# Gated MLP on groups of four token tiles: gate and up matmuls of 512 columns, with tanh and key masks in place

## Chip, cores, metric

One core of a Trainium2 chip (trn2). The metric is device time of one execution in microseconds, the median over runs; lower is better.

## The reference, cut to what matters

Two layers, each of sliding-window attention (32 heads of 16, window 256) and a gated MLP, on 2048 tokens of width 512, in bf16:

```python
def _B_ref(x, w_gate, w_up, w_down):          # F = 1792
    g = x @ w_gate
    u = x @ w_up
    return (sigmoid(g) * u) @ w_down

x = x + A(layernorm(x)); x = x + B(layernorm(x))   # twice, with the same weights
```

The kernel computes sigmoid(g)·u as 0.5·(tanh(g/2) + 1)·u, the 0.5 being applied after the down projection.

## The kernel before

The kernel does not write its instructions in a loop nest. A list scheduler in Python, run once when the kernel is built, plays the engines through with estimated durations and emits each instruction when its turn comes. What remains on the chip is one fixed order for each engine, with semaphores between them. Numbers for tuning (priorities, paces, ranks, slacks) steer that scheduler. TensorE's work comes as "units" that each own one of four PSUM banks until they are evacuated; between them go the "visits" of the attention (scores into a separate buffer, one exponential of 128x2048 each) and the values. The rest, all projections and the gated MLP, is called dense below. xnT is the normalized input and OnT the attention output, both transposed, mostly by DMA, for the matmuls that read them.

The gate and up unit took one or two token tiles of 128. Gate and up shared a bank, 256 columns each:

```python
def gate_up_unit(self, L, t0, n, fcs, chunk):            # n = 1 or 2 tiles
    def steps(bank):
        pt = self.banks[bank][:].rearrange("p (i f w) -> p i f w", i=2, w=w)      # w = n * 128
        return [... nc.tensor.matmul(pt[:, i, j, :], lhsT=wt[:, kt, fc * P:(fc + 1) * P],
                    rhs=self.xnT[key][0][:, c0 // P:(c0 + w) // P, kt, :], start=kt == 0, stop=kt == KT - 1)
                for i, wt in enumerate((self.wg, self.wu)) for j, fc in enumerate(fcs) for kt in range(KT)]
    def evac(u):
        def tanh(e):
            box["th"] = self.take("th")                                           # ring of 3
            nc.scalar.activation(out=box["th"][0][:], in_=pt[:, 0, :], func=AF.Tanh, scale=0.5)
        def mult(e):
            nc.vector.scalar_tensor_tensor(out=self.hT[:, chunk, :], in0=box["th"][0][:], scalar=1.0,
                                           in1=pt[:, 1, :], op0=ALU.add, op1=ALU.mult)
# ... cut
```

Keys were copied from PSUM into one of two `kt` buffers and from there masked into a padded key buffer, once for the even and once for the odd heads:

```python
def cp(e):
    box["kt"] = self.take("kt")
    self.copy(e, box["kt"][0][:], self.banks[u.bank][:])
def split(e):
    for i in range(2):
        nc.vector.tensor_scalar(out=self.kTp[gi % 2][:, cq, :, i, :], in0=box["kt"][0][:]..., scalar1=self.rms[i][:, 0:1], ...)
```

The softmax here doesn't subtract the row's maximum and nothing guards it: scores larger than these inputs give would overflow.

## Time and profile before

| | kernel before |
|---|---|
| time, median of 3 (first measurement) | 545.37 us (545.32 to 545.83) |
| span of the profiled execution | 544.5 us |
| TensorE matmul / weight load / VectorE / ScalarE busy | 98 / 65 / 77 / 72 % |
| granted TensorE clock | full |
| TensorE instructions: matmuls, weight loads | 11,068 of each |

Two groups of the page matter besides (line, engine, operation, output<-input, shapes, count | busy us, mean ns of one | idle time before, and what ended it); they are the evacuation of the gate and up banks in the kernel before:

```profile
L817 ACT ACTIVATE th<-bank 128x256 bf16<-128x256 f32 x224 | 80.6, 386 | 61.6 <-PE bank L805 58.0
L820 DVE SCALAR_TENSOR_TENSOR hT<-th,bank 128x256 bf16<-128x256 bf16 x224 | 87.7, 415 | 36.8 <-ACT th L817 36.0
```

ScalarE stands idle for 58.0 us in total until TensorE has a gate bank ready, and VectorE for 36.0 us until the tanh is there. Neither engine is what TensorE works towards; they follow it.

### The profile page before, as it was taken

How to read it: one execution, taken by the hardware profiler on the slowest of the kernel's cores; microseconds unless marked ns; L12 is line 12 of the kernel's file. 1: busy time of each engine (PE TensorE's matmuls, PEld its weight loads, DVE VectorE, ACT ScalarE, POOL GpSimd, SP SyncE). 2: the span in 40 equal slices, each digit the busy share in tenths (PEclk: the TensorE clock that was granted, in tenths of full speed). 3: DMA queues.
4: the chain of work that ended last, by engine and by line, in shares of the span. 5: the costliest groups of instructions: out<-in, count | busy, mean ns of one | idle time of the engine just before them, and what ended most of it. 6: DMA issues, size and time to landing. Idle time of an engine off the chain costs nothing.

```text
span 544.5 us, 24319 instructions
## 1 busy us (share of the span) xinstructions
PE 534.5 (98%) x11068; PEld 354.8 (65%) x11068; DVE 420.6 (77%) x902; ACT 394.5 (72%) x455; POOL 45.3 (8%) x105
## 2 busy tenths in 40 slices
PE   8999999999999999999999999999999999999997
PEld 7446754866667565665667656766667576777874
DVE  6998989787989889899878877886666867554432
ACT  3999879878889787788878877786878875422321
POOL 6301100010101010001100001010000000000000
PEclk9999999999999999999999999999999999999999
DMA  8852233232313271345111621136111422310000
GB/s 272 312 137 91 42 72 52 63 42 53 61 43 42 52 109 26 60 88 73 37 37 42 109 43 35 35 54 104 42 42 38 85 60 49 63 40 10 12 22 29
DMA packets 94903, 36.41 MB, mean 67 GB/s; under 512 B 78160, under 2 KB 93776, under 8 KB 94800
## 3 DMA queue, kind: packets, MB, share of 16 engines
q1 hardware_dynamic: 93440, 33.56, 29.2%
q8 instruction: 86, 1.41, 1.0%
q10 hardware_dynamic: 1360, 1.31, 0.8%
q14 instruction: 17, 0.14, 0.1%
HBM read 9.70 MB, written 2.10 MB: 22 GB/s over the span
## 4 chain that ended last, share of the span: by engine, by line
PE 91%; DVE 3%; DMA 3%; ACT 2%; issue 1%; POOL 0%; ACTq 0%; POOLq 0%
PE bank L805 35%; PE bank L838 17%; PE bank L1082 9%; PE Sps L1002 7%; PE bank L865 5%; PE bank L713 5%; PE bank L742 5%; PE bank L778 4%; DMA xnT<-xn 2%; PE Sps L1013 2%; PE bank L1265 1%; ACT PTring L1055 1%; ACT edge L1055 1%; DVE edge L933 1%; DMA OnT<-On 1%
## 5 line engine op out<-in xcount | busy, mean ns | idle before, releaser
L1055 ACT ACTIVATE PTring<-Sps 128x2048 bf16<-128x2048 f32 (+1 forms) x122 | 225.9, 1852 | 45.0 <-PE Sps L1002 41.8
L805 PE MATMUL bank<-xnT,wg 128*128 128x256 bf16 (+1 forms) x1064 | 138.1, 256 | 1.4 <-DMA xnT<-xn 0.8
L805 PE MATMUL bank<-xnT,wu 128*128 128x256 bf16 (+1 forms) x1064 | 139.1, 256 | 0.0
L817 ACT ACTIVATE th<-bank 128x256 bf16<-128x256 f32 x224 | 80.6, 386 | 61.6 <-PE bank L805 58.0
L820 DVE SCALAR_TENSOR_TENSOR hT<-th,bank 128x256 bf16<-128x256 bf16 x224 | 87.7, 415 | 36.8 <-ACT th L817 36.0
L838 PE MATMUL bank<-wd,hT 128*128 128x512 bf16 x448 | 115.3, 380 | 0.0
L805 PEld LDWEIGHTS <-wg 128*128 128x128 bf16 x1064 | 89.3, 98 | 28.0 <-issue 2.7
L805 PEld LDWEIGHTS <-wu 128*128 128x128 bf16 x1064 | 90.6, 98 | 11.4 <-issue 0.6
L1055 ACT ACTIVATE edge<-Sps 128x2048 bf16<-128x2048 f32 (+1 forms) x32 | 56.7, 1772 | 12.9 <-PE Sps L1013 12.9
L838 PEld LDWEIGHTS <-hT 128*128 128x128 bf16 x448 | 41.5, 98 | 34.0 <-issue 0.8
L933 DVE TENSOR_TENSOR PTring<-PTring,mask 128x1024 bf16<-128x1024 bf16 x64 | 43.9, 687 | 22.5 <-ACT PTring L1055 22.3
L1082 PE MATMUL bank<-PTring,Vaug 128*32 128x64 bf16 (+1 forms) x2880 | 52.2, 203 | 0.5 <-issue 0.5
L1002 PEld LDWEIGHTS <-kTp 32*128 32x128 bf16 x1984 | 25.6, 93 | 41.0 <-issue 39.2
L1082 PEld LDWEIGHTS <-Vaug 128*32 128x32 bf16 x2880 | 44.1, 97 | 9.7 <-issue 6.4
L1002 PE MATMUL Sps<-qT,kTp 32*128 32x64 bf16 (+3 forms) x1984 | 47.9, 214 | 2.1 <-ACT PTring L1055 2.0
L621 POOL TENSOR_SCALAR st<-st 128x2 f32<-128x2 f32 (+1 forms) x37 | 11.2, 303 | 431.6 <-DVE st L616 431.6
L615 DVE BATCH_NORM_STATS2 st<-xsb 128x6 f32<-128x512 bf16 x64 | 43.9, 686 | 2.1 <-DMA xsb<-in_A_x_dram 1.7
L1082 PE MATMUL bank<-edge,Vl 128*32 128x64 bf16 x1024 | 44.5, 193 | 0.0
L681 DVE CAST OTs<-bank 128x512 bf16<-128x512 f32 x51 | 37.1, 729 | 9.0 <-PE bank L1082 8.8
L933 DVE TENSOR_TENSOR edge<-edge,maske 128x1024 bf16<-128x1024 bf16 x60 | 40.6, 682 | 4.1 <-ACT edge L1055 3.9
L1082 PE MATMUL bank<-edge,Vh 128*32 128x64 bf16 x896 | 40.8, 193 | 0.0
L933 DVE TENSOR_TENSOR PTring<-PTring,maskn 128x1024 bf16<-128x1024 bf16 x56 | 38.1, 682 | 0.7 <-ACT PTring L1055 0.7
(71 smaller groups left out, 527.5 us busy)
## 6 DMA issues: line engine op xcount, KB each, us to landing
Vl<-Vaug SPq DMA_DIRECT2D x32, 68.0 KB, 2.8
out_dram<-xsb SPq DMA_DIRECT2D x16, 128.0 KB, 2.1
Vh<-Vaug SPq DMA_DIRECT2D x28, 68.0 KB, 2.8
wg<-in_B_w_gate_dram SPq DMA_DIRECT2D x2, 896.0 KB, 10.1
wu<-in_B_w_up_dram SPq DMA_DIRECT2D x2, 896.0 KB, 12.8
wd<-in_B_w_down_dram SPq DMA_DIRECT2D x7, 256.0 KB, 4.7
xsb<-in_A_x_dram SPq DMA_DIRECT2D x6, 256.0 KB, 7.0
wq<-in_A_wqkv_dram ACTq DMA_DIRECT2D x2, 256.0 KB, 4.7
```

The source lines that it names most:

```text
L615: nc.vector.bn_stats(out=st[:, 0:6], in_=self.xsb[:, t, :])
L681: self.nc.vector.tensor_copy(out=out, in_=in_)
L713: return [(mm_ns(w), lambda kt=kt, o=o: nc.tensor.matmul(self.banks[bank][:, o:o + w], lhsT=self.wq[:, kt, cq * P:cq * P + P], rhs=self.xn ...
L742: return [(mm_ns(w), lambda kt=kt, o=o: nc.tensor.matmul(self.banks[bank][:, o:o + w], lhsT=self.wq[:, kt, D + cq * P:D + cq * P + P], rhs ...
L805: return [(mm_ns(w), lambda i=i, j=j, fc=fc, wt=wt, kt=kt: nc.tensor.matmul(pt[:, i, j, :], lhsT=wt[:, kt, fc * P:(fc + 1) * P], rhs=self. ...
L817: nc.scalar.activation(out=box["th"][0][:], in_=pt[:, 0, :], func=AF.Tanh, scale=0.5)
L820: nc.vector.scalar_tensor_tensor(out=self.hT[:, chunk, :], in0=box["th"][0][:], scalar=1.0, in1=pt[:, 1, :], op0=ALU.add, op1=ALU.mult)
L838: nc.tensor.matmul(self.banks[bank][:], lhsT=self.hT[:, c, o:o + P], rhs=self.wd[:, fc, :], start=fc == 0, stop=fc == FC - 1)
L933: done = pl.task({"DVE": dve_bf_ns(1024)}, lambda e: nc.vector.tensor_tensor(out=r, in0=r, in1=m.to_broadcast([P, 16, HP]), op=ALU.mult), ...
L1002: nc.tensor.matmul(self.sps[:, m, o:o + n * HP], lhsT=kTp[32 * m:32 * m + 32, i, tt, e, :], rhs=self.qT[32 * m:32 * m + 32, i, q0:q0 + n * ...
L1055: nc.scalar.activation(out=out, in_=src, func=AF.Exp, scale=scale)
L1082: nc.tensor.matmul(o, lhsT=Va[:, c0:c0 + 32], rhs=p(h), start=k == 0 or t == 0, stop=k == len(parts) - 1 or t == 0, tile_position=(0, 32 * g))
```

## The change

The intent: matmuls of 512 columns for gate and up, so that each weight load serves four token tiles. Gate and up then fill a bank each. The tanh is written straight into hT and multiplied there; the key copy goes straight into the padded key buffer and is masked there. Both free buffers, and hT grows from 16 to 28 chunks of 256. The tuning numbers were set anew. Cut to its core:

```diff
-GT = 2
-GW = GT * P
-HCH = 16
+GW = 2 * P
+HCH = 28
+KS = 8
+GLU = [[[1] * 4 + [4], [1] * 4 + [2] * 2, ...], [..., [4] * 4]]     # tiles per group; g0=1, g2=2 choose
-PACE = [2621, 3006, 2091, 2676, 22]
+PACE = [2621, 3006, 2055, 2786, 22]
 ... PRIO, SLACK, RANK, LATE_PRIO, LATE_SLACK, LATE_RANK: new numbers (cut)
-        self.kTp = [big.tile([P, NCQ, NBG, 2, P], BF16, name=f"kTp{i}") for i in range(2)]
+        self.kTp = big.tile([P, NCQ, KS, 2, P], BF16, name="kTp")
-        self.hT = big.tile([P, HCH, GW], BF16, name="hT")
+        self.hT = big.tile([P, HCH * GW], BF16, name="hT")
-        ring("kt", 2, [P, TGW])
-        ring("th", 3, [P, GW])
@@ keys
-                self.copy(e, box["kt"][0][:], self.banks[u.bank][:])
+                    self.copy(e, self.kTp[:, cq, at:at + n, 0, :], self.banks[u.bank][:]...)
-                for i in range(2):
-                    nc.vector.tensor_scalar(out=self.kTp[gi % 2][:, cq, :, i, :], in0=box["kt"][0][:]..., ...)
+                    for i in (1, 0):
+                        nc.vector.tensor_scalar(out=kt[:, :, i, :], in0=kt[:, :, 0, :], ...)
@@ gate and up
+            def tanh(...): nc.scalar.activation(out=self.hT[:, ch[0] * GW:ch[0] * GW + size], in_=pt, func=AF.Tanh, scale=0.5)
+            def mult(...): h = self.hT[:, ...]; nc.vector.scalar_tensor_tensor(out=h, in0=h, scalar=1.0, in1=pt, ...)
+            # four tiles: two units, one bank each
+            units.append(Unit(kind, lambda bank, fcs=fcs: mms(bank, (self.wg,), fcs), needs, True, gate))
+            units.append(Unit(kind, lambda bank, fcs=fcs: mms(bank, (self.wu,), fcs), [], False, up))
```

More of the change, by code (lines that the diff above doesn't have):

```diff
@@ L98 @@
 EXP_NS = 1880
-PACE = [2621, 3006, 2091, 2676, 22]
+GLU = [[[1] * 4 + [4], [1] * 4 + [2] * 2, [1] * 6 + [2], [1] * 8], [[4] * 3 + [2, 1, 1], [4] * 3 + [2, 2], [4] * 4]]
+PACE = [2621, 3006, 2055, 2786, 22]
 EARLY = 12
@@ L113 @@
 FETCH = (1200, 2300)
-PRIO = dict(st_x0=8.84, ap_x0=5.2, xt_x0=4.11, st_x1=6.83, ap_x1=4.97, xt_x1=-3.99, st_x=7.22, ap_x=1.33,
-    xt_x=-1.25, st_p=4.93, ap_p=3.21, xt_p=4.95, st_g=6.44, ap_g=2.28, xt_g=4.79, st_g0=1.93, ap_g0=1.06,
-    xt_g0=2.83, tp=5.29, tp_g=-1.09, q=6.35, q0=3.12, q1=2.88, k=3.53, k0=2.42, k1=4.8, s=-1.61, s0=0.46,
-    s1=0.69, v=-0.71, v0=3.45, v1=8.0, vv=2.2, exp=4.44, exp0=4.73, m0=4.61, m00=-2.03, e0=2.88, e00=6.59,
-    e1=-0.82, e10=4.98, m2=0.81, m20=21.82, th=1.67, mu=-0.98, dn=0.66, add=6.3, add0=5.49, out=5.31, mv=6.94,
-    mv0=3.86, oq=4.47, oq0=3.3, no=1.9, no0=2.41, on=-0.26, on0=4.14, vc=2.28, vc0=5.62)
@@ L122 @@
-OPT = dict(gu='SP', g1=1, bk=1, bq=1, wide=0, r0=2)
-SLACK = dict(xt=1080, oq=1057, on=696, vc=1992)
-RANK = dict(tp=-0.355, o=1.872, lead=10.494, far=6.876, v=1.959, g=2.363, d=3.317, feed=15.682, x3=44361,
-    wd=380, go=211)
-LATE_PRIO = dict(st_p=4.07, ap_p=5, xt_p=3.41, st_x=1.67, ap_x=2, xt_x=-0.8, st_g=2.98, ap_g=0.63, xt_g=2,
-    q=3.84, k=3, s=3, v=3, exp=3, m0=4.57, e0=1.63, e1=6, m2=6.84, th=0.66, mu=1, dn=1.45, add=0.69, out=5.87,
-    mv=5.22, oq=0.1, no=4, on=2, vc=3.04)
-LATE_SLACK = dict(xt=0, oq=0, on=345, vc=0)
@@ L130 @@
-LATE_RANK = dict(tp=-2, o=-1, lead=10, far=5.293, v=4, g=1.974, d=2.5, feed=12, go=300)
+PRIO = dict(st_x0=9.66, ap_x0=5.2, xt_x0=4.11, st_x1=6.83, ap_x1=4.97, xt_x1=-3.99, st_x=7.22, ap_x=1.33,
+    xt_x=-1.25, st_p=4.93, ap_p=3.21, xt_p=5.11, st_g=6.44, ap_g=2.28, xt_g=4.67, st_g0=1.93, ap_g0=2.34,
+    xt_g0=2.83, tp=5.29, tp_g=-2.14, q=6.35, q0=1.85, q1=2.88, k=3.53, k0=0.63, k1=0.73, s=-1.61, s0=0.46,
+    s1=5.56, v=-1.31, v0=3.84, v1=8.0, vv=4.71, exp=4.44, exp0=6.15, m0=4.27, m00=-2.03, e0=3.94, e00=6.05,
+    e1=4.23, e10=4.3, m2=0.81, m20=21.82, th=2.08, mu=-0.98, dn=2.02, add=5.32, add0=5.49, out=5.31, mv=6.36,
+    mv0=3.86, oq=6.63, oq0=3.3, no=0.56, no0=0.37, on=-0.26, on0=4.14, vc=4.31, vc0=-2.12)
@@ new lines @@
+OPT = dict(gu='SP', g1=1, bk=1, bq=1, wide=0, r0=2, g0=1, g2=2)
+SLACK = dict(xt=1080, oq=240, on=28, vc=2480)
+RANK = dict(tp=-2.963, o=1.872, lead=10.494, far=6.876, v=1.959, g=2.363, d=3.317, feed=14.564, x3=44361,
+    wd=12, go=211)
+LATE_PRIO = dict(st_p=4.07, ap_p=2.35, xt_p=6.18, st_x=1.67, ap_x=5.19, xt_x=-0.8, st_g=2.98, ap_g=1.19,
+    xt_g=5.62, q=3.84, k=3, s=3, v=0.28, exp=3, m0=4.62, e0=1.63, e1=6, m2=6.84, th=3.38, mu=3.54, dn=2.85,
+    add=0.69, out=5.87, mv=5.22, oq=0.1, no=4, on=1.28, vc=3.04)
@@ L134 @@
+LATE_SLACK = dict(xt=0, oq=1051, on=203, vc=0)
+LATE_RANK = dict(tp=-2, o=1.5, lead=10, far=5.293, v=1.796, g=1.974, d=2.466, feed=22.042, go=1418)
 class Late(dict):
@@ L732, in q_unit, with k_slots @@
         return u
+    def k_slots(self, j, n):
+        a = min(n, KS - j % KS)
+        return [(0, a, j % KS)] + ([(a, n - a, 0)] if n > a else [])
     def k_unit(self, L, g, cq):
@@ L746, in evac @@
         def evac(u):
-            box = {}
             u.done.then(lambda: self.used(key, 1))
+            slots = self.k_slots(gi * NBG, NBG)
             def cp(e):
-                box["kt"] = self.take("kt")
-                self.copy(e, box["kt"][0][:], self.banks[u.bank][:])
+                for a, n, at in slots:
+                    self.copy(e, self.kTp[:, cq, at:at + n, 0, :], self.banks[u.bank][:].rearrange("p (t k) -> p t k", k=P)[:, a:a + n, :])
             def split(e):
-                for i in range(2):
-                    nc.vector.tensor_scalar(out=self.kTp[gi % 2][:, cq, :, i, :], in0=box["kt"][0][:].rearrange("p (t k) -> p t k", k=P),
-                                            scalar1=self.rms[i][:, 0:1], scalar2=None, op0=ALU.mult)
-            a = pl.task({"ACT": act_ns(TGW), "DVE": dve_ns(TGW)}, cp, [u.done], self.prio["k" + self.phase(L, g)], lambda: self.has("kt"))
-            b = pl.task({"DVE": 620}, split, [a.done], self.prio["s" + self.phase(L, g)], port=True)
-            b.done.then(lambda: (self.give(box["kt"]), self.k_ready[L, g, cq].fire()))
+                for a, n, at in slots:
+                    kt = self.kTp[:, cq, at:at + n]
+                    for i in (1, 0):
+                        nc.vector.tensor_scalar(out=kt[:, :, i, :], in0=kt[:, :, 0, :], scalar1=self.rms[i][:, 0:1], scalar2=None, op0=ALU.mult)
+            a = pl.task({"ACT": act_ns(TGW), "DVE": dve_ns(TGW)}, cp, [u.done], self.prio["k" + self.phase(L, g)])
+            b = pl.task({"DVE": 300 + 320 * len(slots)}, split, [a.done], self.prio["s" + self.phase(L, g)], port=True)
+            b.done.then(self.k_ready[L, g, cq].fire)
             return a.done
@@ L765, in k_unit @@
         needs = [self.has_wq["k"]] + ([] if by_tile else tiles)
-        if gi >= 2:
-            needs.append(self.seen[divmod(4 * (gi - 2) + 3, NT)])
+        if gi * NBG + NBG > KS:
+            needs.append(self.seen[divmod(gi * NBG + NBG - 1 - KS, NT)])
         u = Unit(("k", L, g, cq), steps, needs, False, evac)
@@ L796, in v_unit @@
         return Unit(("v", L, t), steps, needs, False, evac)
-    def gate_up_unit(self, L, t0, n, fcs, chunk):
-        nc, pl, key = self.nc, self.pl, ("g", L, t0 // NBG)
-        c0, w = (t0 % NBG) * P, n * P
-        def steps(bank):
-            pt = self.banks[bank][:].rearrange("p (i f w) -> p i f w", i=2, w=w)
-            return [(mm_ns(w), lambda i=i, j=j, fc=fc, wt=wt, kt=kt: nc.tensor.matmul(
-                pt[:, i, j, :], lhsT=wt[:, kt, fc * P:(fc + 1) * P], rhs=self.xnT[key][0][:, c0 // P:(c0 + w) // P, kt, :],
-                start=kt == 0, stop=kt == KT - 1))
-                for i, wt in enumerate((self.wg, self.wu)) for j, fc in enumerate(fcs) for kt in range(KT)]
-        def evac(u):
-            box = {}
-            u.done.then(lambda: self.used(key, 1))
-            pt = self.banks[u.bank][:].rearrange("p (i w) -> p i w", i=2)
-            def tanh(e):
-                box["th"] = self.take("th")
-                nc.scalar.activation(out=box["th"][0][:], in_=pt[:, 0, :], func=AF.Tanh, scale=0.5)
-            def mult(e):
-                nc.vector.scalar_tensor_tensor(out=self.hT[:, chunk, :], in0=box["th"][0][:], scalar=1.0, in1=pt[:, 1, :],
-                                               op0=ALU.add, op1=ALU.mult)
-            a = pl.task({"ACT": act_ns(GW)}, tanh, [u.done], self.prio["th"], lambda: self.has("th"))
-            b = pl.task({"DVE": dve_ns(GW)}, mult, [a.done], self.prio["mu"])
-            b.done.then(lambda: (self.give(box["th"]), [self.h_ready[L, t0, fc].fire() for fc in fcs]))
-            return b.done
-        needs = [self.xn_ready[key, t] for t in range(t0, t0 + n)] + [self.has_gu]
-        needs.append(self.h_free[chunk])
-        self.h_free[chunk] = self.h_used[L, t0, fcs[-1]]
-        return Unit(("g", L, t0, fcs[0]), steps, needs, True, evac)
@@ L833, in down_unit, with glu_units, mms, tanh @@
-    def down_unit(self, L, t, t0, n, chunks):
+    def glu_units(self, L, t0, n, c0):
+        key, kind = ("g", L, t0 // NBG), ("g", L, t0)
+        q0, w = t0 % NBG, n * P
+        per = GW // w if n < NBG else 1
+        def mms(bank, wts, fcs):
+            pt = self.banks[bank][:, 0:len(wts) * len(fcs) * w].rearrange("p (i f w) -> p i f w", i=len(wts), w=w)
+            return [(mm_ns(w), lambda i=i, j=j, fc=fc, wt=wt, kt=kt: self.nc.tensor.matmul(
+                pt[:, i, j, :], lhsT=wt[:, kt, fc * P:(fc + 1) * P], rhs=self.xnT[key][0][:, q0:q0 + n, kt, :],
+                start=kt == 0, stop=kt == KT - 1))
+                for i, wt in enumerate(wts) for j, fc in enumerate(fcs) for kt in range(KT)]
+        units = []
+        for at, f in enumerate(range(0, FC, per)):
+            fcs = list(range(f, f + per))
+            ch = [(c0 + at * (w * per // GW) + i) % HCH for i in range(w * per // GW)]
+            box = {"got": Event()}
+            needs = [self.xn_ready[key, t] for t in range(t0, t0 + n)] + [self.has_gu]
+            for c in ch:
+                needs.append(self.h_free[c])
+                self.h_free[c] = self.h_used[L, t0, fcs[-1]]
+            size = w * per
+            def tanh(pt, box, done, ch=ch, size=size):
+                def fn(e):
+                    self.nc.scalar.activation(out=self.hT[:, ch[0] * GW:ch[0] * GW + size], in_=pt, func=AF.Tanh, scale=0.5)
+                a = self.pl.task({"ACT": act_ns(size)}, fn, [done], self.prio["th"])
+                a.done.then(box["got"].fire)
+                return a.done
+            def mult(pt, box, done, fcs=fcs, ch=ch, size=size):
+                def fn(e):
+                    h = self.hT[:, ch[0] * GW:ch[0] * GW + size]
+                    self.nc.vector.scalar_tensor_tensor(out=h, in0=h, scalar=1.0, in1=pt, op0=ALU.add, op1=ALU.mult)
+                b = self.pl.task({"DVE": dve_ns(size)}, fn, [done, box["got"]], self.prio["mu"])
+                b.done.then(lambda: [self.h_ready[L, t0, fc].fire() for fc in fcs])
+                return b.done
+            if n < NBG:
+                def evac(u, box=box, tanh=tanh, mult=mult):
+                    u.done.then(lambda: self.used(key, 2))
+                    pt = self.banks[u.bank][:].rearrange("p (i w) -> p i w", i=2)
+                    tanh(pt[:, 0, :], box, u.done)
+                    return mult(pt[:, 1, :], box, u.done)
+                units.append(Unit(kind, lambda bank, fcs=fcs: mms(bank, (self.wg, self.wu), fcs), needs, True, evac))
+                continue
+            def gate(u, box=box, tanh=tanh):
+                u.done.then(lambda: self.used(key, 2))
+                return tanh(self.banks[u.bank][:], box, u.done)
+            def up(u, box=box, mult=mult):
+                u.done.then(lambda: self.used(key, 2))
+                return mult(self.banks[u.bank][:], box, u.done)
+            units.append(Unit(kind, lambda bank, fcs=fcs: mms(bank, (self.wg,), fcs), needs, True, gate))
+            units.append(Unit(kind, lambda bank, fcs=fcs: mms(bank, (self.wu,), fcs), [], False, up))
+        return units
@@ L834, in down_unit @@
+    def down_unit(self, L, t, t0, n, c0):
         nc, pl = self.nc, self.pl
         def mm(bank, fc):
-            c, o = (chunks[fc], (t - t0) * P) if n == 2 else (chunks[fc // 2], fc % 2 * P)
-            nc.tensor.matmul(self.banks[bank][:], lhsT=self.hT[:, c, o:o + P], rhs=self.wd[:, fc, :],
+            o = c0 * GW + fc * n * P + (t - t0) * P
+            o %= HCH * GW
+            nc.tensor.matmul(self.banks[bank][:], lhsT=self.hT[:, o:o + P], rhs=self.wd[:, fc, :],
                              start=fc == 0, stop=fc == FC - 1)
@@ L977, in scores @@
         nc, pl = self.nc, self.pl
-        kTp = self.kTp[(L * NTG + t // NBG) % 2]
-        tt = t % NBG
+        kTp = self.kTp
+        tt = (L * NT + t) % KS
         U = UNIT[L * NT + t]
@@ L1405, in go @@
             self.left["p", L, g] = 2 * NCQ + NBG
-            self.left["g", L, g] = FC * NBG // 2
+            self.left["g", L, g] = FC * NBG
         self.xnT, self.outs, self.oprojs, self.open, self.fed = {}, {}, [], [], set()
@@ L1434, in go @@
             t0 = 0
-            while t0 < NT:
-                k = 1 if L * NT + t0 < 4 or L * NT + t0 >= 2 * NT - 2 else 2
-                m = FC * k // 2
-                chunks = [(c + i) % HCH for i in range(m)]
-                c += m
-                gs += [self.gate_up_unit(L, t0, k, (i,) if k == 2 else (2 * i, 2 * i + 1), chunks[i]) for i in range(m)]
+            for k in (GLU[0][OPT["g0"]] + [4] * 2 if L == 0 else GLU[1][OPT["g2"]]):
+                c += c % 2 if k == NBG else 0
+                gs += self.glu_units(L, t0, k, c)
                 for t in range(t0, t0 + k):
-                    d = self.down_unit(L, t, t0, k, chunks)
+                    d = self.down_unit(L, t, t0, k, c)
                     d.begin = self.down_began[L, t]
                     ds.append(d)
+                c = (c + FC * k // 2) % HCH
                 t0 += k
```

## The prediction

> **What bounds the kernel now.** I read the page first, then the chain of work that ended last in order of time, then the waits of TensorE alone, then its timeline.
>
> ```profile
> span 544.5 us, 24319 instructions
> PE 534.5 (98%) x11068; PEld 354.8 (65%) x11068; DVE 420.6 (77%) x902; ACT 394.5 (72%) x455; POOL 45.3 (8%) x105
> PEclk9999999999999999999999999999999999999999
> PE 91%; DVE 3%; DMA 3%; ACT 2%; issue 1%; POOL 0%; ACTq 0%; POOLq 0%
> ```
>
> TensorE is busy in 98% of the span, at the full clock, and 91% of the chain that ended last is TensorE. A busy matmul row is not yet proof, since rows overlap, so the question is whether matmuls follow each other as closely as they can. The chain in order of time (start, length, what) gives the rates in the dense stretch after the attention is over:
>
> ```profile
> 481.31 3.45 PE bank L838 x16
> 484.76 1.75 PE bank L805 x16
> ...
> 516.10 1.79 PE bank L805 x32
> 517.88 3.45 PE bank L838 x16
> ```
>
> 16 matmuls of 512 columns take 3.45 us (215.6 ns each), 16 of 256 columns 1.75 us (109.2 ns, from the starts of longer runs in the timeline), 32 of 128 columns 1.79 us (55.9 ns). Each step begins where the one before ended. The waits of TensorE alone (engine, line, waited for: us in total, times, longest):
>
> ```profile
> PE Sps L1002 <- ACT PTring L1055: 2.0, 3, 0.8
> PE bank L1265 <- POOL ident L536: 1.4, 1, 1.4
> PE bank L805 <- DMA xnT<-xn: 0.8, 2, 0.7
> PE bank L1082 <- issue: 0.5, 1, 0.5
> PE bank L805 <- DVE hT L820: 0.4, 1, 0.4
> ```
>
> All of them together, with three of 0.2 us, are 5.7 us, of which 1.4 us is the start. ScalarE, by contrast, often waits for TensorE (58.0 us ahead of tanh, 41.8 us ahead of the exponential), and VectorE for ScalarE. They are not the bound.
>
> I then added up TensorE's time from its timeline. It alternates between dense matmuls, scores (four row tiles) and values (four column tiles). Counting from the instruction order: 162 dense stretches, 154 of scores, 63 of values. The dense matmuls at the three rates make 411.9 us. Each dense stretch takes about 0.107 us more than its matmuls (entering the other tile layout), 17.3 us. The stretches of scores take 0.34 us each, 51.7 us in all, those of values 0.81 us, 51.2 us in all. With 1.45 us at the start and 3.8 us from the last matmul to the end, this is 537.4 us; the missing 7.1 us are the half-speed matmuls of the first microseconds (2.7 us) and the waits above (4.3 us). So the span is a sum of TensorE work with under 1% of waiting in it.
>
> **What the Trainium skill says.** "TensorE: Matmul & The Clock Gate", Part 1, "Wait — 56ns, not 53.3ns?": warm matmuls follow each other at N ÷ 2.4 GHz plus some 2.5 ns. The trace agrees: 55.9, 109.2 and 215.6 ns are 2.6, 2.5 and 2.3 ns above 53.3, 106.7 and 213.3. The same page's "Back-to-back issue gap" gives 81 ns at N=128 and 131 ns at N=512 for a stream of weight loads with matmuls; the trace contradicts both (55.9 and 215.6 ns with one weight load per matmul), and the trace decides. "PSUM — Partial Sum Buffer", "The four PSUM rules": one output fits one bank, 512 fp32 columns, so 512 tokens is as far as this widening can go, and it takes a whole bank for gate and another for up. "ScalarE: Activation LUTs", "What ACT_TABLE_LOAD costs": an ACTIVATE with immediate scale takes 186 ns plus 0.833 ns per element, 399 ns at 256; the trace has 386.
>
> **The change, part by part.**
>
> *Wider GLU matmuls.* Before: 6 tiles alone and 13 pairs, so 6·112 = 672 matmuls of 128 columns and 13·112 = 1456 of 256. After (counted in the changed kernel's instruction order): 4 tiles alone, 2 pairs, 6 groups of four, so 448 of 128, 224 of 256 and 672 of 512. The columns are the same; only the number falls, by 784 (and 784 weight loads). At the measured rates: before 672·55.9 + 1456·109.2 = 196.6 us; after 448·55.9 + 224·109.2 + 672·215.6 = 194.4 us. Gain 2.2 us, which is 784 times the fixed cost. All of it is on the path. Down projection, q, k, v, output projection, scores and values have the same counts and widths; the 84 warming matmuls stay too. The weight loads removed (784·98 ns = 77 us of busy weight loading) lie beside matmuls and are worth nothing by themselves.
>
> *Stretches.* In the changed order there are 161 dense stretches for 162, 154 and 63 of the others as before: 0.1 us.
>
> *Tanh and multiply of 512.* Before 224 of each, now 56 of 256 and 84 of 512. ScalarE: the exponential's rows (1880 ns at 2048, 1452 at 1536 elements) give 0.836 ns per element, so a tanh of 512 is 386 + 214 = 600 ns; 224·386 = 86.5 becomes 56·386 + 84·600 = 72.0 us. VectorE: the same operation on 512 is in the page at 689 ns (L847); 224·415 = 93.0 becomes 56·415 + 84·689 = 81.1 us. So 14 and 12 us less work, on engines that wait for TensorE: off the path, worth nothing directly. It makes their waits for TensorE longer.
>
> *In place.* The tanh goes into hT itself, and the key copy goes into the masked key buffer, whose two halves are then multiplied there. The counts stay: 32 copies and 64 multiplications, 128x512 at 351 ns. This saves five buffers, which pay for a longer hT (28 chunks for 16), and removes no instruction. The new key buffer holds eight tiles like the two old ones, and has the same release condition. Nothing on the path.
>
> *Order.* Priorities and paces were tuned again. The dense work after the last scores and values grows from 72.0 to 75.5 us, and that in between them falls from 339.9 to 334.2 us: the attention ends a little earlier, and the sum is what was counted above.
>
> Sum: 2.3 us less on TensorE, plus what happens to the 4.3 us of waits. Fewer instructions of the other engines might take away about a fifth of them, and coarser pieces might bring as much; I take 0.5 us off. The run before takes 545.4 us, so 542.6 us.
>
> **The rivals.**
>
> *Coarser pieces stall the path.* A tanh of 600 ns ahead of an exponential holds it up by 0.2 us longer, and the scores share one buffer with the exponential, so TensorE may wait. For it: in the first layer scores follow each other at about 2.7 us, and 2.38 us is the shortest seen, so there the loop of scores and exponential has only some 0.3 us to spare; a bank is also held for longer by gate and up, and there are four. Against it: exponentials of 1.88 us in a period of 2.7 us leave 0.8 us, in the second layer's 3.1 us even 1.2 us, and a tanh of 600 ns fits; 56 of the 84 wide tanhs belong to the second layer. If half of the 84 cost 0.15 us each, that is 6 us, and the time 549 us.
>
> *The waits go.* With 14 and 12 us less work on ScalarE and VectorE, and a new order, all 4.3 us might vanish: 545.4 - 2.3 - 4.3 = 538.8 us. Against it: three of the waits are for transfers and instruction issue, which the change hardly touches. A gain of 2% (534.5 us) is out of reach even so.
>
> *Weight loads are the bound.* Then 784 fewer would give tens of microseconds. Against it: 98 ns loads are paired with matmuls 55.9 ns apart without slowing them. I give it 1%.
>
> **Range and chances.** The counted 2.3 us is sure within some tenths. The waits go from 0 to about 7 us instead of 4.3, where a tuned order makes the lower side as likely as the upper: 540.2 to 545.0 us, eight times in ten. Faster by over 2% needs 10.9 us, and fixed cost and all waits together give 6.6, so 0.02; slower by over 2% (556.3 us) needs the first rival at double its size: 0.02.
>
> **What would show it right or wrong.** Right: gate and up matmuls of 512 columns 215.6 ns apart; TensorE still at 98%, clock full; 1344 gate and up matmuls; ScalarE and VectorE busy some 14 and 12 us less; tanh of 512 near 600 ns and multiply near 689 ns; waits of TensorE between 3 and 6 us. Wrong: waits of TensorE for the exponential or for hT of several microseconds (first rival), waits under 2 us (second), or wide matmuls closer than 213 ns (third).

## The result, and the profile after

The changed kernel takes **542.5 us** (542.13 to 543.19, 6 runs) against 545.43 us (545.07 to 547.11, 6 runs) of the kernel before in the same rounds: ratio 0.9942, 95% interval 0.9928 to 0.9957. Ratios here are the mean time of one kernel's fast runs over that of the other's of the same rounds, so not quite the ratio of the medians quoted. On another occasion it took 542.61 us against 545.81 us, ratio 0.9935 (experiment e1). Both say about 3 us, or 0.6%, within 2%.

Some 77 matmul records are missing from the profile that was taken with the first result, so I read the profile of the repeat e1, where all 10,284 are there. (The profiles of e5 to e13 lack 63 to 88 such records each; runs of "issue" waits of 0.2 us on dense lines are those holes.) The head of its page, with the line of the chain that ended last:

```profile
span 540.6 us, 22607 instructions
PE 532.3 (98%) x10284; PEld 286.9 (53%) x10284; DVE 410.6 (76%) x815; ACT 384.3 (71%) x374; POOL 44.8 (8%) x105
PE 91%; DVE 5%; DMA 2%; ACT 1%; issue 1%; POOL 1%; SPq 0%; DVEq 0%; ACTq 0%
```

TensorE is as busy as before and still makes 91% of the chain, while the weight loads went from 65% to 53% of the span. The chain in order of time (start us, length us, what), in the dense stretch at the end:

```profile
505.32 0.43 PE bank L869 x2
505.75 3.45 PE bank L810 x16
509.21 0.43 PE bank L869 x2
509.64 3.45 PE bank L810 x16
```

16 gate and up matmuls of 512 columns take 3.45 us, 215.6 ns each, as the down projection's did before. The groups of tanh and multiply:

```profile
L836 DVE SCALAR_TENSOR_TENSOR hT<-hT,bank 128x512 bf16<-128x512 bf16 x84 | 57.4, 683 | 39.9 <-PE bank L810 36.1 <-ACT hT L828 3.6
L828 ACT ACTIVATE hT<-bank 128x512 bf16<-128x512 f32 x84 | 49.8, 596 | 52.1 <-PE bank L810 50.7 <-DVE PTring L964 1.0
```

596 and 683 ns, for 600 and 689 expected. VectorE now waits mostly for the up bank, no longer for the tanh. The longest waits of TensorE (engine, line, for what: us in total, times, longest):

```profile
PE bank L1296 <- POOL ident L535: 1.4, 1, 1.4
PE Sps L1033 <- DVE kTp L761: 0.5, 1, 0.5
PE bank L1113 <- issue: 0.5, 2, 0.3
PE bank L810 <- DMA xnT<-xn: 0.5, 1, 0.5
```

No wait is longer than 0.5 us after the start; all together are 4.1 us, where they were 5.7.

TensorE's time, added up as in the prediction (distances of starts in its timeline):

| us | before | changed (e1) |
|---|---|---|
| dense stretches, whole | 436.3 (162) | 431.9 (161) |
| of that, matmuls by count and rate | 411.9 | 409.7 |
| of that, 0.107 for each stretch | 17.3 | 17.2 |
| of that, the rest: half-speed start and waits | 7.1 | 5.0 |
| scores (154 stretches) | 51.7 | 51.8 |
| values (63 stretches) | 51.2 | 51.7 |
| start and end | 5.2 | 5.2 |
| span | 544.5 | 540.6 |

So of the 3.9 us between these two single executions, 2.2 are counted matmul work, 0.1 a stretch less, and the rest is start and waits, less 0.6 that scores and values took more. (The profiled execution of before took 546.21 us, 0.8 more than its median; between the medians there are 2.9 to 3.2 us.)

### The profile page after: what moved, and what is told of

Its sections match the earlier page's. It is cut to its first block, busy times and chain, and to the rows that moved or that the text cites. A ratio compares the mean times of both kernels' runs of the same rounds, so it can differ in the third digit from the quotient of the medians.

```text
span 540.4 us, 22530 instructions
## 1 busy us (share of the span) xinstructions
PE 525.5 (97%) x10207; PEld 286.8 (53%) x10284; DVE 410.2 (76%) x815; ACT 384.1 (71%) x374; POOL 44.9 (8%) x105
## 4 chain that ended last, share of the span: by engine, by line
PE 89%; DVE 5%; issue 2%; DMA 2%; ACT 1%; POOL 1%; SPq 0%; DVEq 0%; ACTq 0%
PE bank L810 37%; PE bank L869 17%; PE bank L1113 9%; PE Sps L1033 7%; PE bank L896 5%; PE bank L782 4%; PE bank L745 4%; PE bank L712 4%; PE Sps L1044 2%; ACT PTring L1086 1%; DVE kTp L761 1%; DMA xsb<-in_A_x_dram 1%; DMA xnT<-xn 1%; DVE st L614 1%; DVE kTp L680 1%
## 5 line engine op out<-in xcount | busy, mean ns | idle before, releaser
L810 PE MATMUL bank<-xnT,wg 128*128 128x512 bf16 (+2 forms) x672 | 125.9, 309 | 0.7 <-DMA xnT<-xn 0.7
L810 PE MATMUL bank<-xnT,wu 128*128 128x512 bf16 (+2 forms) x672 | 124.3, 308 | 0.1
L836 DVE SCALAR_TENSOR_TENSOR hT<-hT,bank 128x512 bf16<-128x512 bf16 (+1 forms) x140 | 78.6, 575 | 42.4 <-PE bank L810 36.1
L828 ACT ACTIVATE hT<-bank 128x512 bf16<-128x512 f32 (+1 forms) x140 | 68.8, 517 | 52.3 <-PE bank L810 50.9
L869 PE MATMUL bank<-wd,hT 128*128 128x512 bf16 x410 | 102.6, 379 | 2.5 <-issue 1.3
L810 PEld LDWEIGHTS <-wg 128*128 128x128 bf16 x672 | 55.3, 98 | 41.4 <-issue 2.0
L810 PEld LDWEIGHTS <-wu 128*128 128x128 bf16 x672 | 55.9, 98 | 39.4 <-issue 1.0
L620 POOL TENSOR_SCALAR st<-st 128x2 f32<-128x2 f32 (+1 forms) x37 | 13.1, 353 | 427.1 <-DVE st L615 427.1
L680 DVE CAST OTs<-bank 128x512 bf16<-128x512 f32 x48 | 34.9, 727 | 8.3 <-PE bank L1113 8.3
L878 DVE SCALAR_TENSOR_TENSOR xsb<-bank,xsb 128x512 bf16<-128x512 f32 x32 | 21.9, 685 | 21.3 <-PE bank L869 21.3
```

The costliest lines, as they stand in the source:

```text
L680: self.nc.vector.tensor_copy(out=out, in_=in_)
L810: return [(mm_ns(w), lambda i=i, j=j, fc=fc, wt=wt, kt=kt: self.nc.tensor.matmul(pt[:, i, j, :], lhsT=wt[:, kt, fc * P:(fc + 1) * P], rhs= ...
L828: self.nc.scalar.activation(out=self.hT[:, ch[0] * GW:ch[0] * GW + size], in_=pt, func=AF.Tanh, scale=0.5)
L836: self.nc.vector.scalar_tensor_tensor(out=h, in0=h, scalar=1.0, in1=pt, op0=ALU.add, op1=ALU.mult)
L869: nc.tensor.matmul(self.banks[bank][:], lhsT=self.hT[:, o:o + P], rhs=self.wd[:, fc, :], start=fc == 0, stop=fc == FC - 1)
L878: d = pl.task({"DVE": dve_ns(D)}, lambda e: nc.vector.scalar_tensor_tensor(out=self.xsb[:, t, :], in0=self.banks[u.bank][:], scalar=0.5, i ...
```

## The experiments

Two batches of four, then one more of four; each batch on one chip, with 4 to 6 fast runs of each kernel and 11 of the kernel before, all of the same rounds. "Before" means that batch's median. Every kernel here gave correct results.

| run | what | us | before | ratio, 95% interval |
|---|---|---|---|---|
| e1_after | changed kernel, control | 542.61 | 545.81 | 0.9935 (0.9921 to 0.9949) |
| e2_split256 | wide matmuls as 2 of 256 | 546.07 | 545.81 | 1.0004 (0.9987 to 1.0021) |
| e3_split128 | wide matmuls as 4 of 128 | 549.52 | 545.81 | 1.0064 (1.0052 to 1.0077) |
| e4_evac256 | wide tanh and multiply as 2 of 256 | 544.32 | 545.81 | 0.9963 (0.9948 to 0.9978) |
| e5_after_oldtune | changed kernel, old tuning | 554.75 | 546.52 | 1.0146 (1.0123 to 1.0168) |
| e6_before_newtune | kernel before, new tuning | 550.07 | 546.52 | 1.0068 (1.0056 to 1.0081) |
| e7_inplace_alone | kernel before, in-place parts alone | 549.12 | 546.52 | 1.0050 (1.0036 to 1.0065) |
| e8_no_pairs | changed kernel, pairs made a four | 552.68 | 546.52 | 1.0114 (1.0099 to 1.0129) |
| e10_before_pace | kernel before, one pace +1% | 554.86 | 546.98 | 1.0160 (1.0138 to 1.0181) |
| e11_after_pace | changed kernel, one pace +1% | 549.43 | 546.98 | 1.0044 (1.0026 to 1.0063) |
| e12_retuned | changed kernel, tuning by a fresh search | 546.61 | 546.98 | 0.9991 (0.9967 to 1.0014) |
| e13_retuned_no_pairs | e8, tuning by a fresh search | 549.13 | 546.98 | 1.0038 (1.0020 to 1.0055) |

The theory going in: TensorE is saturated, and the gain is the fixed cost of 784 matmuls; ScalarE, VectorE and the in-place work are off the path. The rivals: the gain is relief of ScalarE and VectorE; or it is the new tuning.

**e1, the control.** The changed kernel unaltered.

> The changed kernel once more, as the control of this batch. Both theories: ratio to the kernel before 0.994 to 0.996, some 542.5 us; this only tells how well the 2.9 us repeat on another chip.

Measured 542.61 us, ratio 0.9935. The result repeats.

**e2 and e3, the width taken back.** Only the emission changes; the scheduler still believes in one matmul of 512, so the order of everything stays. The halves are whole accumulation groups, one after the other.

```diff
-   [... matmul(pt[:, i, j, :], lhsT=wt[:, kt, ...], rhs=xnT[:, q0:q0 + n, kt, :], ...) for kt in range(KT)]
+   def piece(i, j, fc, wt, k):                       # s = 2 or 4 pieces; as many steps as before
+       for m in range(k * s, k * s + s):
+           h, kt = divmod(m, KT)
+           a, b = h * NBG // s, (h + 1) * NBG // s
+           matmul(pt[:, i, j, a * P:b * P], lhsT=wt[:, kt, ...], rhs=xnT[:, q0 + a:q0 + b, kt, :], start=kt == 0, stop=kt == KT - 1)
```

> The changed kernel, but each 512-column gate and up matmul of the groups of four is issued as two of 256 columns; plan, banks, tanh and multiply stay as they are. 672 more matmuls and weight loads. Theory (fixed cost per matmul on a saturated TensorE): 672 times 2.5 to 2.8 ns, 1.7 to 1.9 us slower than the control, 544.3 us; two thirds of the gain gone. Rival (the gain comes from fewer and wider evacuations or from the new tuning, and narrow matmuls hide in slack): within 0.4 us of the control.

> The same with four matmuls of 128 columns for each of 512: 2016 more matmuls. Theory: 5.0 to 5.4 us slower than the control, about 547.7 us, three times the step of the split in two. Rival (slack): under 1 us. A second rival (weight loads of 98 ns or the fetching of instructions set the pace once matmuls are 56 ns apart): far more than 5.4 us, 20 us or above[...].

Measured: 3.5 us slower than e1 (for 1.9 expected), and 6.9 us slower (for 5.4). The chain in order of time of e2, and then of e3, in the dense stretch at the end:

```profile
516.34 3.49 PE bank L817 x32
```

```profile
516.30 3.57 PE bank L817 x64
```

The same columns take 3.45, 3.49 and 3.57 us as 16, 32 and 64 matmuls: 2.5 ns for each matmul more. And between e2 and e3, which differ by 1344 matmuls, the whole kernel differs by 3.45 us, 2.6 ns each (counted from the three rates: 3.5 us; the spread of the runs leaves some 0.6 ns either way). The slope is the fixed cost. 64 weight loads of 98 ns would take 6.3 us one after the other; they overlap each other and the 3.57 us of matmuls, so loads do not set the pace. What the count did not have is about 1.5 us on top, in both. TensorE's timeline of e2 shows 0.9 us of it, in the one profile of it:

```profile
316.12 0.19 PE L1125 MATMUL bank<-edge,Vh 128*32 128x64 bf16 x1
316.72 0.21 PE L1125 MATMUL bank<-edge,Vh 128*32 128x64 bf16 x3 [0.41 <-issue]
...
362.15 0.41 PE L1056 MATMUL Sps<-qT,kTp 32*128 32x64 bf16 x31
363.03 0.20 PE L1056 MATMUL Sps<-qT,kTp 32*128 32x64 bf16 x1 [0.47 <-issue]
```

TensorE stops in the middle of a run of tiny matmuls that wait for nothing. In the order of its instructions the two places are rows 14,267 and 16,315: exactly 8 times 256 apart. The shorter stalls of this kind in e1 (0.2, 0.3 and 0.3 us) and in the kernel before (0.5 and 0.2 us) lie within two rows of the same place in a block of 256. Instructions come in transfers of 16,384 bytes: 80 of them in e1, 85 in e2, 96 in e3 and 86 in the kernel before, one for each 256 rows of TensorE (20,570, 21,914, 24,602 and 22,138). So a narrow matmul costs its 2.5 ns and a 128th of an instruction transfer, and where such a transfer arrives late, TensorE waits. In e2 the stretches of scores and values take 1.5 us more than in e1 (52.2 + 52.8 against 51.8 + 51.7), and in e3 about as much. With only the width undone and all else left, the time is that of the kernel before: the width carries the gain, in this order.

**e4, the evacuation taken back.** Matmuls and order stay:

```diff
-    self.nc.scalar.activation(out=self.hT[:, ...size], in_=pt, func=AF.Tanh, scale=0.5)
+    for o in range(0, size, GW):
+        self.nc.scalar.activation(out=self.hT[:, ... o ... + GW], in_=pt[:, o:o + GW], func=AF.Tanh, scale=0.5)
     (and the multiply in the same way)
```

> The changed kernel, but each tanh of 512 and each multiply of 512 is issued as two of 256 (84 more of each); matmuls, banks and the plan's order are untouched. This takes back the 14 us of ScalarE and 12 us of VectorE that the change saves. Theory (off the path): within 0.5 us of the control. Rival (the gain is relief of ScalarE and VectorE): back towards the kernel before, 1.5 to 3 us slower than the control.

Measured 1.7 us slower than e1 (the spread of the runs leaves some 0.8 to 2.8): beyond what the theory allows, and within what the rival said. The tail is the dense work after the last scores and values. The waits for OnT in the window of the tail (463 to 542 us) of e4, and in that of e1 (461 to 540 us), where only the weight load waits and no matmul does:

```profile
PE bank L898 <- DMA OnT<-On: 0.8, 1, 0.8
```

```profile
PEld L896 <- DMA OnT<-On: 0.3, 1, 0.3
```

The last output projection of the attention stands in TensorE's fixed order with little time to spare, and the tail is 76.7 us long instead of 75.7. But slower evacuation is not what made its input late. The transpose of OnT is issued 9.1 us after the last values in both (at 472.01 us in e4, at 470.03 in e1); what differs is how long it took to land. The DMA view of 472 to 476 us in e4, then of 470 to 474 us in e1 (last column: us to landing):

```profile
q14 instruction: 1, 0.01, 0.5%
OnT<-On SPq DMA_TRANSPOSE x1, 3.4
```

```profile
OnT<-On SPq DMA_TRANSPOSE x1, 2.5
```

In e4 an instruction transfer (of q14, which brings other engines' instructions) ran while the transpose's packets were moving, in e1 none; e4 has 168 instructions more on those engines. Another 1.0 us of the 2.9 us between the two profiled executions was lost at the start: the first exponential begins at 14.85 us in e4 and at 13.86 in e1, before any gate and up matmul (0.5 and 0.6 us in e2 and e3). And no wait of TensorE for a tanh or a multiply shows in e4. So the 1.7 us is measured, but that the relief of the two engines is worth it is not shown: what the profile shows is moved instruction transfers and a different start.

**e5 and e6, the tuning exchanged.** All of PRIO, OPT, SLACK, RANK, their late versions and PACE swapped between the two kernels:

```diff
 e5 (changed kernel):  -PACE = [2621, 3006, 2055, 2786, 22]   +PACE = [2621, 3006, 2091, 2676, 22]   and the old PRIO, SLACK, RANK ...
 e6 (kernel before):   the reverse
```

> The changed kernel's structure with the priorities, paces, slacks and ranks of the kernel before. Counted from its order: the same dense sum of 409.7 us, 164 dense stretches for 161. Theory (the width gives 2.2 us, the tuning under 1 us): 542.5 to 544 us. Rival (the tuning is the gain): 545 us or more.

> The kernel before with only the new priorities, paces, slacks and ranks. Same matmuls as before, 162 dense stretches, 64 of values for 63. Theory: no gain, 545 to 547 us, as tuned for another kernel. Rival (the tuning is the gain): 542.5 to 543.5 us.

Both expectations fell. e5 takes 554.75 us, 8 us more than the kernel before, though it has the same matmuls as the changed kernel and only three dense stretches more; e6 takes 550.07 us, 3.6 us more than with its own tuning. The tuning is not the gain, since it makes the kernel before slower. But it is a condition of it: each of the two did better with the order chosen for it. The longest waits of TensorE in e5 are

```profile
PE Sps L1033 <- ACT PTring L1086: 3.6, 5, 1.5
PE bank L745 <- DMA xnT<-xn: 3.4, 1, 3.4
```

**e7, the in-place parts alone**, in the kernel before:

```diff
-    self.copy(e, box["kt"][0][:], ...)                     +    self.copy(e, self.kTp[gi % 2][:, cq, :, 0, :], ...)
-    for i in range(2): tensor_scalar(out=kTp[..i..], in0=kt)   +    for i in (1, 0): tensor_scalar(out=kTp[..i..], in0=kTp[..0..])
-    activation(out=box["th"][0][:], ...)                   +    activation(out=self.hT[:, chunk, :], ...)
```

> The kernel before with one part of the change alone: the tanh written into hT and multiplied there, the key copy written into the masked key buffer and masked there; five buffers fewer. Its TensorE order has the same counts. Theory: same time as the kernel before within 0.5 us. Rival (buffers of the tanh or of the keys cause waits that in-place work removes): 1 to 3 us faster.

Measured 2.6 us slower than the kernel before, in all six runs. This is not the cost of the instructions: the masking takes 351 ns as before, tanh 386, multiply 415, and TensorE's order is the same, instruction by instruction. What changed are the waits: 2.9 us for the transpose OnT, 0.2 before. The same transpose, by the issues of a window of 5 us in e7 and in the kernel before (to landing in us, the last column):

```profile
OnT<-On SPq DMA_TRANSPOSE x1, 4.3
```

```profile
OnT<-On SPq DMA_TRANSPOSE x1, 2.4
```

Both windows hold one instruction transfer. In e7 it runs while the transpose's packets are moving; in the kernel before it starts 0.7 us after the last of them. TensorE waits 1.56 us in e7 for that landing. (Single transposes took up to 4.3 us in the kernel before too; there TensorE did not stand behind them.) The pair is no accident. In the 14 kept profiles, 221 transposes of OnT have a recorded landing and no other data transfer beside them. 144 of them had no instruction transfer while their packets moved, and landed within 2.4 to 2.7 us; 77 had one, and took 2.7 to 4.5 us, 3.4 in the median. The waits of TensorE for OnT of 1.2 and 1.6 us in e12, and of 0.8 and 1.6 us in e6, stand behind such transposes too. That is a regularity of the traces; no run here moved an instruction transfer alone. Which of the two in-place parts moved the timing I did not separate. The other direction, the changed kernel with its two `kt` buffers put back, does not fit: the build refuses it, as it needs 209.25 KB per partition of 207.87. The in-place work is what pays for 28 chunks of hT, and that is its worth.

**e8, taken further**: `g0=1` to `g0=0`, a group of four in place of the two pairs.

> The changed kernel taken further: in the first layer the two pairs of tiles become a group of four too, so 28 tiles of 32 go in fours. Another 112 matmuls fewer: dense sum 409.4 us for 409.7, one dense stretch more. Theory: 0.3 us less from the fixed cost, plus or minus 1 us of waits as nothing was tuned for it: 541.5 to 543.5 us. If the group of four is held back by its last tile in the first layer, it costs more: 544 us or above.

Measured 552.68 us, 10 us slower than the changed kernel. Its first-layer group does wait for a transposed input (2.2 us, from 147.5 to 149.7 us; the transpose took 5.0 us to land, with an instruction transfer in its time), so the second reading of the expectation holds as far as that. e13 shows how much of it was the order.

**e10 and e11, one number moved by 1%**: `PACE = [2621, ...]` to `[2647, ...]`, in the kernel before and in the changed one.

> The kernel before with one tuning number moved by 1%: the pace of the first layer's visits, 2621 to 2647. Same matmuls, 165 dense stretches for 162 (0.3 us). Theory (each tuned order sits in a narrow good spot, since a fixed order that drifts by some 0.1 us runs transfers into instruction fetches): 1 to 4 us slower than the kernel before. Rival (the order hardly matters, and what e5 to e8 lost has other causes): within 0.7 us of it.

> The same 1% step in the changed kernel, 163 dense stretches for 161. Theory: 1 to 4 us slower than the changed kernel, 543.5 to 546.5 us, so the same move may hide the whole gain. If the order hardly matters: 542.5 to 543.2 us. Against e10: if width is worth its 2.2 us under both orders, this stays 1 to 4 us ahead of e10; if it is not, they tie.

Measured 7.9 us slower for the kernel before, and some 6 us for the changed one (which was not in these rounds: ratio 1.0044 against 0.9935 in e1). The 4 us that I expected at most is exceeded in both, and it is more than the change is worth. Under the moved pace the changed structure is ahead by 5.4 us, under the tuned orders by 3. The timeline of e10 at its worst place, from 217 to 224 us:

```profile
217.46 1.23 SPq L1101 DMA_TRANSPOSE Oq<-OTs  x1
...
222.42 0.35 DVE L1136 RECIPROCAL Rt<-Oq 128x32 f32<-128x32 bf16 x1 [3.82 <-DMA Oq<-OTs]
222.81 0.69 DVE L1137 TENSOR_TENSOR On<-Oq,Rt 128x512 bf16<-128x512 bf16 x1
223.42 0.41 DVE L820 SCALAR_TENSOR_TENSOR hT<-th,bank 128x256 bf16<-128x256 bf16 x1
```

and TensorE's next matmul after the values in the same timeline:

```profile
223.89 1.01 PE L805 MATMUL bank<-xnT,wg 128*128 128x256 bf16 x4 [2.06 <-DVE hT L820]
```

A transpose lands 4.9 us after its issue (the median is 3.3), with an instruction transfer of each kind and other transfers in its time. VectorE takes its instructions in order and stands 3.82 us before the reciprocal that needs it. The multiply that would free a gate and up bank is behind it in the queue, so TensorE stands 2.06 us for a bank. Then comes a second cost. Stretches of the same profile: the window, then busy time of each engine, and the granted TensorE clock, third from the end:

```profile
222.00:224.00 2.00, 0.11 (x1) 0.10 (x1) 1.54 (x4) 0.59 (x1) 0.00 (x0) 0.93 0.13 38
224.00:226.00 2.00, 2.00 (x11) 1.35 (x10) 1.70 (x4) 0.21 (x1) 0.00 (x0) 0.50 0.33 66
226.00:228.00 2.00, 2.00 (x29) 1.35 (x28) 0.42 (x1) 1.18 (x3) 0.00 (x0) 0.72 0.04 8
228.00:230.00 2.00, 2.00 (x89) 1.64 (x90) 1.57 (x4) 1.29 (x5) 0.00 (x0) 1.00 0.00 0
```

After 2 us without work the clock falls to half, for some 3.4 us ((0.07·2 + 0.50·2 + 0.28·2)/0.5). That loses another 1.7 us: the wait costs almost twice its length. e5 (after its wait of 3.4 us), e8, e11 and e13 have such a place too; the kernel before and the changed one have none between the start and the end. In e11 a wait of 1.9 us was enough; in e8 and e13 two waits within some 5 us of each other (1.7 and 1.0, 0.9 and 2.4 us) brought half clock for 6.8 us. Single waits of up to 1.6 us (e6, e7, e12) brought none.

**e12 and e13, tuned again**: the changed kernel and e8 with numbers from a random search that shortened the scheduler's own estimate.

> The changed kernel's structure with priorities, paces and ranks from a fresh random search, so another order of the same instructions. Same counts: dense sum 409.7 us, 161 dense stretches, tail 75.0 us. Theory: nothing can be gained beyond the 4 us of waits that remain, 538.5 us at best; 540 to 546 us, as the waits of an order show on the chip only. Rival (tuning is worth far more than counted work): below 538 us.

> e8 (28 tiles in fours) with an order of its own from the same search: dense sum 409.4 us, 158 dense stretches, 153 of scores and 60 of values, so 0.7 us less of counted work than the changed kernel. Theory (e8 lost its 10 us by its untuned order, not by its groups): most of e8's loss comes back, 540 to 546 us. Rival (the early group of four itself waits for its last tile): 550 us or above again.

e12 takes 546.61 us, outside its expected range by less than its runs spread (544.1 to 547.8), and some 3 us worse than the changed kernel (ratio 0.9991 against 0.9935), though its counted work is the same; TensorE waits 2.9 us for OnT again. e13 gets back some 4 of e8's 10 us. It has the least counted TensorE work of all and is still slower than the kernel before. No run was faster than the changed kernel.

## Why the prediction was right, point by point

- **The bound and the sum.** Right. The fixed cost of 784 matmuls (2.5 to 2.8 ns each, so 2.0 to 2.2 us) is in the trace of e1, and e2 and e3 give 2.6 ns for each matmul on the chip. e2 alone, undoing only the width, brings the time of the kernel before back.
- **Waits, 0.5 us off.** Right in size: some 0.6 to 0.9 us of the 2.9 to 3.2 between the medians are left after 2.3 counted. This was a guess and stays one, and that the total came out within 0.1 us is luck: single executions of the kernel before differ by up to 2 us (545.07 to 547.11).
- **Weight loads are worth nothing.** Right as to their 98 ns. But the prediction did not see that 1568 fewer rows are also six instruction transfers fewer, and that a late one stops TensorE for 0.4 to 0.5 us (e2). As a gain they do not show: such stalls add up to 0.7 us in the profile of before and 0.8 us in that of e1.
- **Tanh and multiply.** The durations were right (596 for 600, 683 for 689). The relief was 10 us on each engine, where I said 14 and 12: I had multiplied count by mean, and rows of one engine overlap (224·386 ns is 86.5 us, the page's busy time 80.6).
- **"Off the path, worth nothing directly."** Not borne out by the time, and open as to the cause. e4 lost 1.7 us where this allows 0.5. Its profile shows no wait of TensorE for a tanh or a multiply; it shows a transpose that landed 0.9 us later, with an instruction transfer in its time, on a chain with next to no slack. The step missed that instructions off the path also move transfers.
- **In place, nothing on the path.** True of the instructions, as their durations show. The part alone made the kernel before 2.6 us slower (e7), by moved timing. In the tuned order of the changed kernel that doesn't appear.
- **New order.** The prediction counted from the order that the changed kernel really has, and that is why it came out. Its silent step, that another order would give about the same, is false: by the ratios e5, e6, e10, e11 and e12 are some 3 to 11 us from their tuned twin with the same matmuls.
- **The rivals.** Coarser pieces did not stall the path: TensorE waits 0.2 us for the exponential where it was 2.0. The waits went only in part, 4.1 of 5.7 us being left. Loads as the bound is out by e3.

Open: how much of the 2.9 us is the width by itself, free of any order. Counted it is 2.2, undone alone it is 3.5 (e2), with the pace moved in both it is 5.4. The count is the only one of these in which no order plays a part. The parts undone singly (3.5 us in e2, 1.7 in e4) add up to more than the gain, so they are not shares of it. And e12, another tuned order of the changed kernel, ties with the kernel before (0.9967 to 1.0014): how much of the 2.9 us a luckier search found, on either side, stays untested.

## What to carry to other kernels

Where TensorE is saturated, a change of width is in itself worth the difference of its counted matmuls at their measured distances, and that can be worked out to some tenths of a microsecond beforehand: here 2.5 to 2.8 ns for each matmul saved at the same columns. What the whole kernel gains depends on its order too. In a kernel with a fixed, tuned order, test a part of a change with the order held (as in e2 to e4), because a new order alone moved the time here by 3 to 11 us, one to four times the gain. Even a held order does not hold the instruction transfers: an edit that adds instructions moves them (e2, e4). And look for TensorE waits near 2 us first: here they cost the clock as well.

## What the Trainium skill lacked or had wrong

- "TensorE: Matmul & The Clock Gate", "Back-to-back issue gap", gives 81 ns at N=128 and 131 ns at N=512 for weight load and matmul pairs. These runs show 55.8 ns (64 in 3.57 us, e3), 109.1 ns (32 in 3.49 us, e2) and 215.6 ns (16 in 3.45 us, e1), which is the page's own formula for an isolated matmul.
- The same page, "Why this matters for your kernels", warns of TensorE gaps over some 3 us. In e10 a gap of 2.06 us and in e11 one of 1.86 us were enough for half the clock during some 3.4 us.
- "Advanced Engine Details and Errata", "ISA Cache", has lines of 16 KB with 256 instructions, and the runs agree (16,384-byte transfers, 80 for 20,570 rows, stalls 8·256 rows apart). No page has a figure for what a late line costs: waits of 0.41 and 0.47 us in e2. Nor has one the transfer's company with DMA transposes (OnT landed after 2.4 to 2.7 us in 144 cases without an instruction transfer among its packets, after 3.4 us in the median of 77 with one).
- "TensorEngine Tiling (Array Packing)", "Key Properties", says that changing the tiling mode drains TensorE, without a figure. Here each dense stretch between scores or values takes 0.107 us more than its matmuls, 17 us of the whole kernel and eight times what the change gains by width.
